# Chunk-selected attention and a gated feed-forward layer on one core: scores of the first batch's four head pairs in two halves of query rows, and a DMA turn for the norm rows of its second half

## The chip, the cores and the metric

The kernel runs on one core of a Trainium2 chip. The metric is the time of one execution on the device in microseconds (us), as the median of several runs; lower is better. A core has five engines that work side by side, each in its own fixed order: TensorE (PE, matrix products and transposes), VectorE (DVE), ScalarE (ACT), GpSimd (POOL) and SyncE (SP, which here only issues DMAs). DMA engines move data between DRAM and the on-chip memory SBUF. Matrix products land in PSUM, a small memory of eight banks.

## The reference: what is computed

There are 4 batches, 8 heads, 768 positions and a head dimension of 64. The first part is attention in which every query row keeps only six chunks of 32 keys, chosen by an upper bound on the scores:

```python
k_min, k_max = min and max of k over each chunk of 32 keys
ub = np.sum(np.maximum(q * k_min, q * k_max), axis=-1)      # per query row and chunk
ub = np.where(causal, ub, -1e9)
top_chunks = np.argsort(ub, axis=-1)[..., -6:]
scores = q @ k.T / np.sqrt(64), masked to top_chunks and to the past
attn = softmax(scores)
x = attn @ v                                               # heads side by side: 3072 x 512
```

The second part works on the 3072 rows of x:

```python
xn = x / sqrt(mean(x * x) + 1e-6) * rms_g
g, val = xn @ w_gate, xn @ w_val                            # 512 -> 1536
out = (g / (1 + exp(-g)) * val) @ w_out                     # 1536 -> 512
```

## The kernel before, in words

The attention part goes by pairs of heads: four pairs a batch, sixteen in all (pair p belongs to batch p // 4). The 768 rows of a pair are six tiles of 128.

*Preparation of a pair* (`prep`). Queries and keys are loaded, turned on TensorE (`kT`, `qT`; the tiles pk and pq, line 525) and copied out of PSUM by ScalarE or VectorE (`kE`, `qE`). VectorE takes chunk minima and maxima (`kmn`, `kmx`), an engine takes relu of the turned queries (`relu`, line 641 or 643), and TensorE multiplies them to the bounds (`ub`, line 731; from pair 6 on two pairs together, line 789). The bounds are copied out (`ubE`), turned back (`up`), masked (`ubm`), and the sixth largest is found (`max`, `sel`). What is selected stands as extra rows beside the queries, so that one product gives the masked scores. For pairs 0 to 2 these rows are turned by TensorE (`selT`, `selC`); from pair 3 on they go through a buffer `qn` of bf16 queries and are turned by DMA from SP's queue (`qX`). The two `qn` buffers are cleared once by VectorE (`qn0`, line 356). POOL casts keys to bf16 (`kC`) and issues the loads of values and of the feed-forward weights wg, wv and wo.

*Scores* (`scores`). The causal triangle of a head is 21 blocks of 128 x 128. They come in groups of at most four blocks: TensorE makes a group of scores (`sc`, line 876; in the first batch also adds the triangular mask, line 882), ScalarE takes the exponentials (`exp`, line 893), TensorE multiplies them with the values (`av`, line 912). When all groups of a head are done, VectorE divides by the sums and writes the rows to xb (`xb`, lines 932 and 933). A pair is done whole (six groups a head) or in two halves of 384 query rows, with two groups for the first half (4 and 2 blocks) and four for the second (4, 4, 4 and 3). Which of the two is set by `PARTS`; before, only pair 3 goes in halves.

*Norm and feed-forward* (`norm`, `ffn`). Both go by halves of a batch, 384 rows. The norm sums squares (`sq`, on ScalarE or VectorE), takes the root on POOL (`root`, line 981), scales the rows on VectorE (`xs`, line 989) and turns them: in batch 0 by TensorE (`tp`, line 1011) with a copy out of PSUM (`tpE`), in the other batches by a DMA from SP's queue (`xT`, line 1000). The feed-forward has twelve groups of four gate matmuls (gp, line 1045), each followed by tanh on ScalarE (line 1052) and a product on VectorE (`tg`), twelve of four val matmuls (vp, line 1066) with another product (`hh`), and nine groups of four output matmuls (po, line 1086).

*Fillers.* `busy` (line 346) emits matmuls on a tile of zeros that nothing reads: 48 of 512 columns from the start on and 40 of 256 columns once the last scores of pair 2 are out (`BUSY, LATER = 48, 40`).

*Order.* Every piece of work is a step with an engine, an assumed duration, a rank and the buffers it opens and uses. A planner in the kernel (`Order.run`) goes through assumed time and gives each free engine the ready step of lowest rank whose buffers are free. The ranks are sums of table entries: `RANK` by kind of step (first batch, later batches), `TIMES` by the place in the problem (s0.3 is the second half of the scores of pair 0, n0.1 the norm of the second half of batch 0, f0.1 its feed-forward). Fillers have the highest ranks, so TensorE gets one when nothing else of its own is ready in assumed time. The result is one fixed order an engine. On the chip each engine follows its order and waits where an input or a buffer is not ready.

Of the kernel before, what the change touches and what calls it, by code (L numbers as in the profile page):

```python
# [26 lines left out]
    dict(  # L27
        av=439.71, dif=-349.0, eps=-276.35, exp=56.9, kC=119.11, kE=221.89, kT=-479.5,
        kload=-91.99, kmn=-561.73, kmx=-221.73, max=-117.69, qC=120.39, qE=644.67, qN=97.14,
        qT=303.27, qX=110.23, qload=17.43, relu=-156.64, root=392.56, sc=392.96, sel=176.91,  # L30
        selC=388.0, selT=-168.59, sq=-325.5, tp=-47.15, tpE=460.17, ub=-387.44, ubE=-1000.64,
        ubm=-238.37, up=-379.03, vload=-360.06, xb=-167.37, xs=293.02,
    ),
    dict(
        av=-243.01, dif=-122.81, eps=-968.41, exp=80.0, gate=-57.45, hh=-33.27, kC=474.21,
        kE=54.78, kT=-28.02, kload=327.35, kmn=571.37, kmx=673.95, mask=-6.85, max=351.72,
        out=-338.93, po=268.25, poE=188.61, qE=-4.14, qN=444.8, qT=271.57, qX=-691.62,
        qload=314.07, relu=202.91, root=-1348.37, sc=-186.72, sel=354.08, sq=285.76, tanh=579.3,
        tg=-259.04, ub=-101.04, ubE=-390.25, ubm=307.49, up=-117.99, val=-52.48, vload=103.56,
        xT=119.23, xb=-299.83, xs=-84.52,  # L40
    ),
)

TIMES = {
    "a0": -417.11, "a1": 120.7, "a10": 211.74, "a11": -52.39, "a12": 226.13, "a13": 390.87,
    "a14": 307.84, "a15": 583.2, "a2": -326.55, "a3": -12.31, "a4": -161.66, "a5": -30.78, "a6":
    133.0, "a7": 70.59, "a8": 128.02, "a9": 121.26, "f0.0": 33.65, "f0.1": 8.37, "f1.0": -84.59,
    "f1.1": 458.33, "f2.0": 528.25, "f2.1": 57.29, "f3.0": 75.85, "f3.1": 711.78, "ke": 138.67,
    "ke0": 432.93, "l0": -295.48, "l1": -95.28, "l10": 399.97, "l11": 344.28, "l12": 487.92,
    "l13": 531.58, "l14": 907.9, "l15": 667.8, "l2": 140.89, "l3": 25.16, "l4": -81.25, "l5":  # L50
    119.09, "l6": 9.37, "l7": 156.16, "l8": 243.85, "l9": 217.21, "n0.0": -794.06, "n0.1":
    230.63, "n1.0": -549.93, "n1.1": 453.35, "n2.0": -334.87, "n2.1": 123.71, "n3.0": 67.64,
    "n3.1": 574.2, "pace0": -0.69, "pace1": 11.25, "pacef0.0": 0.39, "pacef0.1": 15.72,
    "pacef1.0": 11.97, "pacef1.1": 14.19, "pacef2.0": 25.48, "pacef2.1": 21.31, "pacef3.0":
    -30.15, "pacef3.1": 4.73, "pacen": -9.51, "qn0": -62.11, "s0.0": -763.02, "s1.0": -94.31,
    "s10.0": 453.73, "s11.0": -82.75, "s12.0": 288.69, "s13.0": 337.03, "s14.0": 103.21,
    "s15.0": 675.54, "s2.0": -261.49, "s3.0": -328.04, "s3.3": -46.56, "s4.0": -161.4, "s5.0":
    -551.5, "s6.0": 217.9, "s7.0": -246.19, "s8.0": -166.64, "s9.0": 57.52, "step": 1.25, "w":
    26.4, "w0": -49.72, "w1": -9.78, "w2": 75.1, "w3": 187.17,
}  # L60
# [141 lines left out]
def kernel(  # L202
# [11 lines left out]
    nc = tc.nc  # L214
# [5 lines left out]
    NT = S // P  # L220
# [23 lines left out]
    WHOLE, HALVES = [(0, NT)], [(0, HB), (HB, HB)]  # L244
    PARTS = [WHOLE] * 3 + [HALVES] + [WHOLE] * (NPAIRS - NP)
    FIRST = 42.0
# [7 lines left out]
    def add(name, engs, occ, rank, *a, **kw):  # L254
        return order.add(name, engs, occ, rank if isinstance(rank, dict) else {"": rank}, *a, **kw)
# [93 lines left out]
    for i in range(BUSY):  # L349
# [3 lines left out]
            for i in range(SLOTS["ku"])]  # L353
    c_sel = [add("selq0", "DVE", 0.38, -90 + i, lambda e, i=i: nc.vector.memset(SELQ[i][:], 0.0))
             for i in range(SLOTS["selq"])]
    c_qn = [add("qn0", "DVE", 0.5, {"qn0": 1.0}, lambda e, i=i: nc.vector.memset(QN[i][:], 0.0))
            for i in range(SLOTS["qn"])]
# [129 lines left out]
    def prep(c, i0, nb, at, lr):  # L487
# [162 lines left out]
        def choose(last, ubm, m8):  # L650
            for j in range(0, nb, 3):
                def top(e, j=j):
                    if m8.tile is None:
                        tile_of(m8, [P, 2, NT, 8] if side_q else [P, NT, 2, 8], FP32, "m8")
                    for x in range(j, j + 3):
                        for h in range(2):
                            y = (h, x) if side_q else (x, h)
                            nc.vector.max(out=m8.tile[:, y[0], y[1], :],
                                          in_=ubm.tile[:, y[0], y[1], 0:max(8, 4 * (i0 + x) + 4)])

                last = add("max", "DVE", 0.33 + 0.05 * j, rank(at, b, "max", j, "step"), top, last, opens=[m8], uses=[ubm])
                last = [last]
# [188 lines left out]
    def scores(c, i0, nb, at, pace, adds):  # L851
# [3 lines left out]
        for hl in range(2):  # L855
# [63 lines left out]

            if p == 2 and hl:  # L920
                for i in range(LATER):
                    bank = Buf("ps")
                    add("busy", "PE", pe(2 * P), 1000.0 + i, busy(bank, 2 * P), [last_sc], opens=[bank])
# [21 lines left out]
    def norm(b, half, at, pace):  # L945
# [38 lines left out]
        for j, i in enumerate(rows):  # L984
# [10 lines left out]

            if b:
                def move(e, i=i, xs=xs):
# [123 lines left out]
    for b in range(B):  # L1121
        for half in range(2):
            norm(b, half, f"n{b}.{half}", "pacen")
            ffn(b, half, f"f{b}.{half}", f"pacef{b}.{half}")
    PLACE.update(TIMES)

# [32 lines left out]
```

## Time and profile before

| | before |
|---|---|
| median of 3 runs | 316.25 us (315.89 to 316.34) |
| the profiled execution | 315.79 us, of which its span is 314.0 us |
| TensorE busy | 308.6 us (98%) |
| VectorE busy | 230.7 us (73%) |
| ScalarE busy | 194.4 us (62%) |
| POOL busy | 100.7 us (32%) |
| granted TensorE clock | 1.0 |
| moved by DMA | 35.36 MB |

A row of the groups view names line, engine and operation, then output<-inputs, the shapes and the count; behind the bar stand the busy time and the mean duration of one, and the idle time just before them with what ended it. A row of the timeline has start and duration (both us), engine, line, operation, count, and in brackets the idle time ahead of it and what ended that. Neighbouring instructions of one kind are merged. Matmuls overlap in the pipeline, so their cost is the distance from start to start, not the duration of one. A row of the windows view gives length and then, for TensorE, its weight loads, VectorE, ScalarE and POOL, the busy time with the count, then clock, DMA share and GB/s. A row of the chain gives start, length and the work that the end of the kernel depends on at that moment. Line numbers are those of the kernel before.

### The profile page before, as it was taken

The page shows a single profiled execution, that of the slowest core. Times are in us where ns is not written, and L with a number is a line of the kernel's source. Part 1 is how long each engine was busy: PE and PEld are TensorE (multiplying, and loading weights), DVE is VectorE, ACT ScalarE, POOL GpSimd, SP SyncE. Part 2 cuts the span into 40 slices and gives each one's busy share as a digit, 9 for nine tenths or more (in the row PEclk, how much of TensorE's full clock was granted, in tenths as well). Part 3 has the DMA queues.
Part 4 walks back from the last instruction along what each step waited for, and adds up shares of the span by engine and source line. Part 5 has one row for each costly group of instructions (what it writes and reads, how often), then busy time and mean ns, then how long its engine had stood idle before and what let it go on. Part 6 is the DMA issues. An engine that isn't in the chain of part 4 may idle for free.

```text
span 314.0 us, 7640 instructions
## 1 busy us (share of the span) xinstructions
PE 308.6 (98%) x2844; PEld 196.1 (62%) x2844; DVE 230.7 (73%) x654; ACT 194.4 (62%) x420; POOL 100.7 (32%) x157
## 2 busy tenths in 40 slices
PE   7999999999999999999999999999999999999995
PEld 4567877666566775666667565656666645655542
DVE  7699986888988487967986799879464663873530
ACT  5589987863475987478579654344988823333321
POOL 8666534342353564045357300001522220000000
PEclk9999999999999999999999999999999999999999
DMA  8999989989989898979934640002341045001102
GB/s 171 210 190 178 145 108 207 198 114 143 196 86 199 126 179 152 201 164 222 158 79 61 93 102 0 2 2 52 84 94 59 20 118 150 3 0 65 38 22 111
DMA packets 113301, 35.36 MB, mean 113 GB/s; under 512 B 106224, under 2 KB 110064, under 8 KB 113264
## 3 DMA queue, kind: packets, MB, share of 16 engines
q1 hardware_dynamic: 83152, 26.62, 40.9%
q0 software_dynamic: 28512, 7.87, 25.6%
q10 hardware_dynamic: 1600, 0.39, 0.6%
q8 instruction: 22, 0.36, 0.5%
q14 instruction: 15, 0.12, 0.1%
HBM read 28.57 MB, written 6.29 MB: 111 GB/s over the span
## 4 chain that ended last, share of the span: by engine, by line
PE 97%; DMA 1%; ACTq 0%; ACT 0%; issue 0%
PE gp L1045 20%; PE vp L1066 20%; PE po L1086 20%; PE sc L876 12%; PE av L912 7%; PE busy L346 4%; PE pq L525 4%; PE pk L525 3%; PE ub L789 2%; PE ub L731 2%; DMA qnat<-in_q_dram 1%; PE up L811 1%; PE sc L882 1%; PE up L755 1%; PE tp L1011 0%; ACTq L505 0%
## 5 line engine op out<-in xcount | busy, mean ns | idle before, releaser
L893 ACT ACTIVATE pt<-sc 128x512 bf16<-128x512 f32 (+2 forms) x192 | 88.4, 578 | 10.1 <-PE sc L876 5.3
L1052 ACT ACTIVATE sg<-gp 128x384 bf16<-128x384 f32 x96 | 47.7, 500 | 62.7 <-PE gp L1045 60.0
L1066 PE MATMUL vp<-xT,wv 128*128 128x384 bf16 x384 | 77.0, 326 | 0.0
L1045 PE MATMUL gp<-xT,wg 128*128 128x384 bf16 x384 | 76.2, 326 | 0.0
L1086 PE MATMUL po<-wo,hh 128*128 128x512 bf16 x288 | 69.3, 379 | 0.0
L1058 DVE SCALAR_TENSOR_TENSOR tg<-sg,gp 128x384 bf16<-128x384 bf16 x96 | 52.2, 548 | 21.7 <-ACT sg L1052 19.5
L1074 DVE TENSOR_TENSOR hh<-vp,tg 128x384 bf16<-128x384 f32 x96 | 51.8, 551 | 11.1 <-PE vp L1066 7.3
L1045 PEld LDWEIGHTS <-wg 128*128 128x128 bf16 x384 | 36.8, 98 | 24.5 <-issue 1.0
L1066 PEld LDWEIGHTS <-wv 128*128 128x128 bf16 x384 | 36.9, 98 | 24.1
L876 PE MATMUL sc<-qs,ke 128*128 128x128 bf16 (+5 forms) x420 | 51.4, 251 | 0.0
L1086 PEld LDWEIGHTS <-hh 128*128 128x128 bf16 x288 | 27.6, 98 | 27.5
L301 POOL CAST ke<-kt 64x768 bf16<-64x768 f32 x31 | 26.4, 852 | 36.9 <-ACT kt L297 17.0
L876 PEld LDWEIGHTS <-ke 128*128 128x128 bf16 (+1 forms) x420 | 30.3, 97 | 11.3 <-issue 1.6
L899 POOL TENSOR_SCALAR_AFFINE_SELECT pt<-pt 128x512 bf16<-128x512 bf16 (+1 forms) x48 | 24.4, 527 | 37.6 <-ACT pt L893 37.4
L912 PEld LDWEIGHTS <-pt 128*128 128x128 bf16 x672 | 28.8, 98 | 7.7 <-POOL ke L301 0.6
L912 PE MATMUL av<-vx,pt 128*128 128x65 bf16 x672 | 32.6, 193 | 0.0
L299 ACT ACTIVATE osb<-po 128x512 f32<-128x512 f32 x19 | 11.4, 602 | 21.4 <-PE po L1086 21.4
L346 PE MATMUL busy<-zeros 128*128 128x512 bf16 (+1 forms) x88 | 20.1, 349 | 1.3 <-DVE zeros L341 1.3
L933 DVE TENSOR_TENSOR xb<-av,rden 128x384 bf16<-128x384 f32 (+1 forms) x34 | 18.1, 534 | 1.2
L989 DVE SCALAR_TENSOR_TENSOR xs<-xb,ri,gains 128x512 bf16<-128x512 bf16 x24 | 16.9, 746 | 2.7 <-DMA xT<-xs 2.1
L301 POOL CAST qn<-qnat 128x768 bf16<-128x768 f32 x10 | 8.2, 821 | 31.9 <-DMA qs<-qn 30.7
L481 POOL DMA_DIRECT2D vx<-in_v_dram x16 | 16.8, 1052 | 4.0 <-PE av L912 2.6
(87 smaller groups left out, 303.1 us busy)
## 6 DMA issues: line engine op xcount, KB each, us to landing
out_dram<-osb SPq DMA_DIRECT2D x24, 256.0 KB, 2.2
knat<-in_k_dram SPq DMA_DIRECT2D x30, 192.0 KB, 4.3
qnat<-in_q_dram SPq DMA_DIRECT2D x30, 192.0 KB, 4.8
vx<-in_v_dram POOLq DMA_DIRECT2D x16, 192.0 KB, 4.7
wg<-in_moe_w_gate_dram POOLq DMA_DIRECT2D x2, 768.0 KB, 8.6
wv<-in_moe_w_val_dram POOLq DMA_DIRECT2D x2, 768.0 KB, 7.8
wo<-in_moe_w_out_dram POOLq DMA_DIRECT2D x2, 768.0 KB, 9.9
qs<-qn SPq DMA_TRANSPOSE x26, 3.3
```

Source lines behind the costliest of these rows:

```text
L301: engine[e].tensor_copy(out_, in_)
L346: nc.tensor.matmul(t[:, 0:n], zeros[:, 0:P], zeros[:, 0:n], start=True, stop=True)
L876: nc.tensor.matmul(t[:, x:x + m, :].rearrange("p a b -> p (a b)"), ke[kk, kb * P:(kb + 1) * P], qs[kk, q0 * P:(q0 + m) * P], start=not tri ...
L893: nc.scalar.activation(out=t[:, 0:nn, :], in_=sc.tile[:, 0:nn, :], func=ACT.Exp, scale=SCALE)
L899: nc.gpsimd.affine_select(out=pt.tile[:, 0:nd, :], in_=pt.tile[:, 0:nd, :], compare_op=ALU.is_ge, fill=0.0, base=0, pattern=[[0, nd], [1, ...
L912: nc.tensor.matmul(av.tile[:, qi - i0, :], pt.tile[:, x, :], VX[c.v.slot][:, hl * NT + kb, :], start=(begin and m == 0), stop=(left[0] == ...
L1045: nc.tensor.matmul(t[:], wg[:, g, hs], XT[b].tile[:, g, cols], start=(g == 0), stop=(g == NP - 1))
L1052: nc.scalar.activation(out=t[:], in_=gp.tile[:], func=ACT.Tanh, scale=0.5)
L1058: nc.vector.scalar_tensor_tensor(out=t[:], in0=sg.tile[:], scalar=1.0, in1=gp.tile[:], op0=ALU.add, op1=ALU.mult)
L1066: nc.tensor.matmul(t[:], wv[:, g, hs], XT[b].tile[:, g, cols], start=(g == 0), stop=(g == NP - 1))
L1074: nc.vector.tensor_tensor(out=t[:], in0=vp.tile[:], in1=tg.tile[:], op=ALU.mult)
L1086: nc.tensor.matmul(po.tile[:], hhs[ht].tile[:, th * P:(th + 1) * P], wo[:, ht, :], start=(ht == 0), stop=(ht == NHT - 1))
```

## The change: what it does

All four pairs of batch 0 now go in two halves. The 40 later fillers wait for the last score group of the second half of pair 2. The norm rows of the second half of batch 0 are turned by DMA from SP's queue instead of by TensorE. The planner's assumed durations of clearing a `qn` buffer and of a group of maxima are raised, the places s0.3, s1.3 and s2.3 are added, and nearly every number in the two tables of ranks is another, so the order of work on all engines differs:

```diff
-        ubm=-238.37, up=-379.03, vload=-360.06, xb=-167.37, xs=293.02,
+        ubm=-390.61, up=-397.31, vload=-301.28, xT=220.85, xb=-318.72, xs=172.54,
...
-    -30.15, "pacef3.1": 4.73, "pacen": -9.51, "qn0": -62.11, "s0.0": -763.02, "s1.0": -94.31,
...
+    -28.83, "pacef3.1": 4.77, "pacen": -12.12, "qn0": -204.68, "s0.0":
+    -858.36, "s0.3": 4.94, "s1.0": -170.21, "s1.3": 225.32, "s10.0": 486.07, "s11.0": -198.16,
+    "s12.0": 334.79, "s13.0": 615.55, "s14.0": -53.83, "s15.0": 697.68, "s2.0": -148.98, "s2.3":
+    74.37, "s3.0": -357.45, "s3.3": 122.85, "s4.0": -43.33, "s5.0": -909.96, "s6.0": 328.66,
...
-    PARTS = [WHOLE] * 3 + [HALVES] + [WHOLE] * (NPAIRS - NP)
+    PARTS = [HALVES] * NP + [WHOLE] * (NPAIRS - NP)
...
-    c_qn = [add("qn0", "DVE", 0.5, {"qn0": 1.0}, lambda e, i=i: nc.vector.memset(QN[i][:], 0.0))
+    c_qn = [add("qn0", "DVE", 0.85, {"qn0": 1.0}, lambda e, i=i: nc.vector.memset(QN[i][:], 0.0))
...
-                last = add("max", "DVE", 0.33 + 0.05 * j, rank(at, b, "max", j, "step"), top, last, opens=[m8], uses=[ubm])
+                last = add("max", "DVE", 0.40 + 0.05 * j, rank(at, b, "max", j, "step"), top, last, opens=[m8], uses=[ubm])
...
-            if p == 2 and hl:
+            if p == 2 and hl and i0 + nb == NT:
                 for i in range(LATER):
...
-            if b:
+            if b or half:
                 def move(e, i=i, xs=xs):
...
+    for p in range(NP - 1):
+        PLACE[f"s{p}.3"] = TIMES[f"s{p}.0"] + 20.0
     PLACE.update(TIMES)
```

In the built order VectorE clears the two `qn` buffers ahead of the zeros tile. Two fillers stand before the first transposes instead of six, and nine of the narrow fillers stand among the score groups of pair 4, behind the first six gate groups. POOL issues the first wo load ahead of the first wv load, and the latter behind the key casts of pair 7.

## The prediction

> **What bounds the kernel now.** I read the page first: busy shares, the slices, and the chain that ended last.
>
> ```profile
> PE 308.6 (98%) x2844; PEld 196.1 (62%) x2844; DVE 230.7 (73%) x654; ACT 194.4 (62%) x420; POOL 100.7 (32%) x157
> PE   7999999999999999999999999999999999999995
> PEclk9999999999999999999999999999999999999999
> PE 97%; DMA 1%; ACTq 0%; ACT 0%; issue 0%
> L346 PE MATMUL busy<-zeros 128*128 128x512 bf16 (+1 forms) x88 | 20.1, 349 | 1.3 <-DVE zeros L341 1.3
> ```
>
> TensorE is busy from the first slice to the last, at full granted clock, and 97% of the chain is TensorE. But 88 of its instructions are fillers, matmuls on a tile of zeros whose result nobody reads. So the stretch before the first gate matmul is not useful work all through; there other engines set the pace and the fillers take up the waiting. The waits of TensorE come next, then the timeline of TensorE and VectorE at the start.
>
> ```profile
> PE busy L346 <- DVE zeros L341: 1.3, 1, 1.3
> PE pq L525 <- DMA qnat<-in_q_dram: 0.3, 1, 0.3
> ```
> ```profile
> 0.93 0.27 DVE L341 MEMSET zeros<- 128x256 uint32 x1 [0.93 <-PEq L1143]
> 1.26 2.74 PE L346 MATMUL busy<-zeros 128*128 128x512 bf16 x6 [1.26 <-DVE zeros L341]
> 2.52 1.75 DVE L356 MEMSET qn<- 128x896 uint32 x2
> 3.79 0.85 PE L525 MATMUL pk<-ident_f,knat 128*128 128x128 f32 x3
> 4.75 0.52 PE L525 MATMUL pk<-ident_f,knat 128*128 128x128 f32 x3
> 9.62 0.65 PE L731 MATMUL ub<-qt,ku 64*32 64x256 f32 x12
> ```
>
> TensorE has only two recorded waits, both before 6 us. After that it issues without a recorded pause until the end. The six fillers from 1.26 to 3.79 take 0.42 each, and the later ones half of that (0.216, below): the first 3.5 us of TensorE's activity run at half rate.
>
> Last the stage where the first gate matmul runs, in the chain and the timeline.
>
> ```profile
> 9.69 1.01 PE ub L731 x24
> ...
> 12.89 2.59 PE busy L346 x12
> ...
> 25.05 1.04 PE av L912 x34
> ...
> 57.87 0.88 PE sc L876 x10
> ...
> 80.00 0.66 PE pk L525 x6
> ...
> 85.21 1.45 PE ub L789 x32
> ```
> ```profile
> 51.08 0.39 PE L1011 MATMUL tp<-ident_b,xs 128*128 128x128 bf16 x4
> 51.30 0.60 PE L346 MATMUL busy<-zeros 128*128 128x256 bf16 x4
> 51.74 0.39 PE L1011 MATMUL tp<-ident_b,xs 128*128 128x128 bf16 x4
> 53.81 2.44 PE L1045 MATMUL gp<-xT,wg 128*128 128x384 bf16 x14
> 55.76 2.11 PE L1045 MATMUL gp<-xT,wg 128*128 128x384 bf16 x12
> 58.59 0.81 PE L1066 MATMUL vp<-xT,wv 128*128 128x384 bf16 x4
> ...
> 61.91 0.81 PE L1066 MATMUL vp<-xT,wv 128*128 128x384 bf16 x4
> ```
>
> The first gate matmul starts at 53.81, and every filler lies ahead of it. Three groups of four fill 53.81 to 55.76, so a gate group takes 0.65; a val group has the same shape. From there to the end TensorE does nothing but useful work. So the time is: the moment T of the first gate, plus all TensorE work behind it, plus whatever TensorE then waits. No later slack exists to absorb a delay.
>
> **The change, part by part.** Where I say what stands where in the new kernel, it is read from its built instructions, engine by engine, which hold no times. The count and widths of the fillers stay: 48 of 512 columns, 40 of 256. That limits the gain at once: a filler is paid whether it covers a wait or not.
>
> *Scores in halves.* A head's exponentials cover the same 21 blocks of 128 in six instructions either way, so ScalarE gains nothing. Score matmuls become 12 more, with the same columns: TensorE 0. Each of six heads of pairs 0 to 2 is normalised twice instead of once:
>
> ```profile
> 42.95 0.17 DVE L932 RECIPROCAL rden<-av 128x3 f32<-128x3 f32 x1
> 43.16 0.36 DVE L933 TENSOR_TENSOR xb<-av,rden 128x192 bf16<-128x192 f32 x1
> 44.40 0.20 DVE L932 RECIPROCAL rden<-av 128x6 f32<-128x6 f32 x1
> 44.63 0.56 DVE L933 TENSOR_TENSOR xb<-av,rden 128x384 bf16<-128x384 f32 x1
> ```
>
> Two halves are 1.06, a whole 0.76: 0.30 x 6 = 1.8 us more on VectorE. In the new order three bound evictions and a mask copy leave VectorE for ScalarE, which more than pays for it, and all first-half rows are normalised before the last second-half scores, so I cost it at nothing. If that cover fails, up to 1.8 goes into T.
>
> *Start.* VectorE now clears the two qn buffers (1.75) ahead of the zeros tile. The zeros are ready at 0.93 + 1.75 + 0.27 = 2.95 instead of 1.20, TensorE's first filler starts near 3.0, and only two run before the first transposes, which stay near 3.8 because the key load sets them. Half rate then lasts to about 6.5. The second key transposes (0.33 at full rate) take 0.64 behind a cold filler and end near 5.56 instead of 5.1; ScalarE's copy and the bounds matmul of pair 0 (9.62) follow. Between 0 (hidden behind another input) and 0.6 (two transposes at double time), I take 0.35.
>
> *Between that bounds matmul and the gate.* Before: 66 fillers, after: 61. Four more are wide (2.59 / 12 = 0.216), nine fewer narrow (51.74 - 51.30 = 0.44 for four, 0.11): +0.86 - 0.99 = -0.13. The rest is equal work (the transposes of pair 7's keys change places with pair 5's queries, 0.66 each). So T = 53.81 + 0.35 - 0.13 = 54.03, if other engines keep up as before.
> Do they? The TensorE work in this stretch adds up to: 22 transposes of 0.33, five bounds of 1.01 and five turns of 0.33, three selection turns (taken like those), 216 score and mask blocks of 0.055 (0.88 / 16), 168 products of 0.031, three turns of 0.22 and 9.98 of fillers, 42.7 us in 53.81 - 9.62 = 44.2. So TensorE loses 1.5 us in small pieces. Bounds on T: 1.5 earlier, or 1.8 later by the VectorE price.
>
> *Behind the gate.* Nine narrow fillers now stand between the scores of pair 4: +0.98. Twelve transposes of the second norm half go to the DMA: three times 51.30 - 51.08 = 0.22, -0.66, with one eviction each off ScalarE or VectorE, which were not the bound.
>
> *A wait that appears.* In the old order the twelve score groups of pair 4 alternate with four val matmul groups (the first and last vp rows stand above), so TensorE works while ScalarE takes the exponentials. In the new one the first wv load is issued only behind the key casts of pair 7 on POOL, and the order puts six gates, then the twelve score groups with nine fillers and two query transposes, then the bounds of pairs 6 and 7, and val only behind these. The bounds wait for the relu of pair 7, and ScalarE has that behind six tanh and ten exponentials:
>
> ```profile
> 57.26 0.49 ACT L1052 ACTIVATE sg<-gp 128x384 bf16<-128x384 f32 x1 [0.16 <-PE gp L1045]
> 57.91 0.49 ACT L1052 ACTIVATE sg<-gp 128x384 bf16<-128x384 f32 x1 [0.16 <-PE gp L1045]
> 58.30 4.68 ACT L893 ACTIVATE pt<-sc 128x512 bf16<-128x512 f32 x10
> 36.54 0.84 ACT L641 ACTIVATE rt<-qt 128x768 f32<-128x768 f32 x1
> ```
>
> The same six tanh and ten exponentials stand in the old order. Each tanh waits for its gate (0.65 apart), and the ten end at 62.98, T + 9.17. The relu ends 0.7 to 0.84 later, so the bounds can start at about T + 10.0. TensorE has until then 6 x 0.65 + 42 x 0.055 + 0.98 + 0.66 = 7.85. It stands 2.15 us, and val, gates and every po queue behind it in order. That is the main term. A lower bound is 0.5 (if ScalarE ran its 6 x 0.49, 4.68 and 0.84 without a pause from the end of the first gate, T + 0.65, the bounds would start at T + 9.1, less 0.7 of overlapping ends), an upper one 3.5 (the two rmsnorm sums that now sit on ScalarE between the last eviction and the first tanh, 0.7 each, fully on the path).
>
> *The turn by DMA.*
>
> ```profile
> xT<-xs SPq DMA_TRANSPOSE x18, 2.4
> wv<-in_moe_w_val_dram POOLq DMA_DIRECT2D x2, 768.0 KB, 7.8
> 119.76 3.83 SPq L1000 DMA_TRANSPOSE xT<-xs  x3
> 49.30 2.78 SPq L505 DMA_DIRECT2D knat<-in_k_dram  x2
> ```
>
> On SP's queue the first turn follows pair 7's query load, then come pair 9's key load (2.78) and two more turns (1.3 each). Issued from about T + 5, they land near T + 5 + 1.3 + 2.8 + 2.6 + 2.4 = T + 14.1. The gates that read them start at 10.0 + 1.45 + four val groups 2.6 + two turns 0.66 = T + 14.7: hidden, with 0.6 to spare, thanks to the stall in front. Between 0 and +2.4 (one landing), I take 0. The queries and keys queued behind (pairs 9 and 5) are used ten microseconds later or more. The wv load, issued near T + 0 (a wo load now goes ahead of it on POOL's queue, some 15 us earlier) and 7.8 long, makes T + 11.5 with 3 us to spare.
>
> *Sum.* +0.35 - 0.13 + 0.98 - 0.66 + 2.15 = +2.7 us. The profiled execution took 315.79 (span 314.0 and 1.8 around it), 0.46 below the median of 316.25. So 318.5 for a profiled run, and 318.95 against the median.
>
> **A rule against the trace.** After its idle start TensorE ran at half rate from the first filler (1.26) to the second key transposes (4.75): 3.5 us, worth 1.75. What gap brings the half rate back, the trace can't show, for it has no gap that long later. The Trainium skill, "TensorE: Matmul & The Clock Gate", section "HAM oscillation — how this bites in real kernels", says that idle gaps over about 3.4 us put the matmul clock back to half. By that rule the forecast's gap adds nothing, and the gap at its upper bound adds the last rival below.
>
> **Rivals.** Measured differences under 0.2% (0.63 us) can't be told from no change.
>
> *No stall (about 316.8).* If ScalarE reaches the relu as TensorE reaches the bounds, what remains is +0.35 - 0.13 + 0.98 - 0.66 = +0.54. For it: ScalarE's earlier idle. Against it: the 0.16 idle before each tanh shows them bound to the gates, and the order of ScalarE is fixed.
>
> *Faster (about 315.0).* First-half rows of all pairs are ready earlier, so the norm chain no longer ends the stretch ahead of the gate, and the 1.5 us lost there in pieces vanish. With a stall of less than about 0.3 that gives 316.25 + 0.54 - 1.5 = 315.3, or 315.0 if the start costs nothing. It decides only if the stall is nearly absent.
>
> *A second full engine (about 320.5).* In the new order 36 exponentials of pairs 5, 9 and 8 run one after another on ScalarE, six heads at 2.55 (4.68 covers nine long ones and a short one), 15.3, with a relu, a sum and four copies some 18 us, in a stretch that holds 18.3 us of TensorE work by the units above. The densest stretch of before:
>
> ```profile
> 100.00:120.00 20.00, 20.00 (x213) 13.77 (x211) 13.95 (x31) 17.76 (x42) 11.31 (x17) 1.00 1.08 169
> ```
>
> ScalarE was 89% busy there and TensorE full. Near 98% each hand-over shows, and 1 to 2 us of waits would come on top.
>
> *Late rows (about 320.8).* If a turn by DMA lands a whole 2.4 late, the first gates of the second half wait 1.8.
>
> *Half rate again (about 322.1).* If the gap at pair 4 is at its upper bound of 3.5 and TensorE falls back to half rate as at the start: 316.25 + 0.54 + 3.5 + 1.75. It needs both rmsnorm sums on the path; T's early norm chain speaks against that.
>
> **How the numbers follow.** The forecast, one stall near 2 us: 46%. No stall: 16%, its times lying on both sides of 316.88, half same, half slower. Faster: 12%. Second engine full: 14%. Late rows: 8%. Half rate: 4%. That gives 0.12 faster, 0.08 same, 0.80 slower. The predicted time is 318.9. The range leaves out most of the faster case and the tail beyond the upper rivals: 316.0 to 321.6. The likeliest case's own range is 317.8 (half the stall) to 320.2 (stall at its upper bound).
>
> **What would show it.** The zeros memset should end near 2.95 and the first filler follow; the first gate should stand at 53.5 to 54.6; in the waits of TensorE a new row should name the bounds (L789 moved by the edit) waiting for ScalarE's relu, about 2 us; nine fillers should lie behind the gate; three more turns by DMA, twelve fewer tp matmuls. I am wrong if TensorE runs from the gate to the bounds in under 8.3 us, if T lies under 53 or over 55.5, or if a wait later than 80 us is longer than the one at pair 4.

## The result, and the profile after

The kernel after takes 319.81 us in the median of four executions (318.35 to 320.34), beside 316.22 (four, 315.89 to 316.34) before: a ratio of 1.0114, with a 95% interval of 1.0097 to 1.013. It is slower, and its own executions spread over 2.0 us where those of before spread over 0.45. The profiled execution of after took 319.87 (span 318.2), that of before 315.79: 4.08 us more.

First lines of the page of after: busy time, the granted clock, the chain, the fillers.

```profile
PE 308.3 (97%) x2823; PEld 197.1 (62%) x2844; DVE 234.2 (74%) x665; ACT 192.7 (61%) x417; POOL 102.4 (32%) x158
PEclk9999999999999999999999999999999999999999
PE 94%; ACT 2%; DMA 2%; issue 1%; DVE 1%; SPq 0%; ACTq 0%
L347 PE MATMUL busy<-zeros 128*128 128x512 bf16 (+1 forms) x87 | 20.8, 347 | 3.2 <-DVE zeros L342 3.1
```

TensorE's busy time and its clock have not moved. What is new is in the chain, where TensorE went from 97% to 94%: the loss is time in which TensorE waits. The view of TensorE's waits names the places:

```profile
PE busy L347 <- DVE zeros L342: 3.1, 1, 3.1
PE pq L526 <- DMA qnat<-in_q_dram: 1.6, 1, 1.6
PE ub L790 <- ACT rt L642: 0.3, 1, 0.3
```

The third row is the wait that the forecast was built on. Its 0.3 counts only from the modelled end of the matmul ahead; by the starts of the matmuls, below, the wait costs 1.23. The second row was not in the forecast. The timeline shows the first two places, the start and the stage behind the first gate:

```profile
1.06 1.75 DVE L357 MEMSET qn<- 128x896 uint32 x2 [1.06 <-PEq L1146]
2.81 0.27 DVE L342 MEMSET zeros<- 128x256 uint32 x1
3.14 1.03 PE L347 MATMUL busy<-zeros 128*128 128x512 bf16 x2 [3.14 <-DVE zeros L342]
10.67 0.65 PE L732 MATMUL ub<-qt,ku 64*32 64x256 f32 x12
```
```profile
54.58 4.06 PE L1046 MATMUL gp<-xT,wg 128*128 128x384 bf16 x24
59.06 4.68 ACT L894 ACTIVATE pt<-sc 128x512 bf16<-128x512 f32 x10
62.71 1.15 PE L790 MATMUL ub<-qt,ku 64*32 64x384 f32 x16
63.38 0.93 PE L790 MATMUL ub<-rt,ku 64*32 64x384 f32 x8
63.51 0.96 ACT L642 ACTIVATE rt<-qt 128x768 f32<-128x768 f32 x1
64.61 0.85 PE L790 MATMUL ub<-rt,ku 64*32 64x384 f32 x8 [0.30 <-ACT rt L642]
65.39 1.47 PE L1067 MATMUL vp<-xT,wv 128*128 128x384 bf16 x8
```

The first bounds come at 10.67 instead of 9.62, and the first gate at T = 54.58 instead of 53.81. ScalarE ends the relu of pair 7 at 64.47, T + 9.9, as forecast. But TensorE does not stand still until then: 24 of the 32 bounds matmuls read the queries, or the relu of pair 6, and go ahead. Only eight wait. Without the wait the 32 take 1.45 and the values would start at 64.16; they start at 65.39, so the stall is 1.23 and not 2.15.

The place that the forecast missed is in batch 1, at the transposes of pair 14's queries (timelines of TensorE and of SP's queue):

```profile
144.63 0.81 PE L1046 MATMUL gp<-xT,wg 128*128 128x384 bf16 x4
147.09 0.52 PE L526 MATMUL pq<-ident_f,qnat 128*128 128x128 f32 x3 [1.64 <-DMA qnat<-in_q_dram]
```
```profile
134.75 5.53 SPq L1001 DMA_TRANSPOSE xT<-xs  x3
140.38 0.53 SPq L1102 DMA_DIRECT2D out_dram<-osb  x1
141.00 1.06 SPq L506 DMA_DIRECT2D qnat<-in_q_dram  x2
```

SP's queue issues in order. The load of pair 14's queries stands behind three norm turns of batch 1, whose issue took 5.53 here, and an output. The queries land near 147, and TensorE, in order too, has val and gate work behind the transposes that need them.

Against the profiled execution of before, the difference is made up so: T +0.77; nine fillers and stall +0.98 + 1.23; transposes that left TensorE -0.66; pair 14 +1.64. The sum is +3.96 of 4.08.

### The profile page after: what moved, and what is told of

It reads as the page before. It is cut to its first block, busy times and chain, and to the rows that moved or that the text cites. A ratio compares the mean times of both kernels' runs of the same rounds, so it can differ in the third digit from the quotient of the medians.

```text
span 318.2 us, 7636 instructions
## 1 busy us (share of the span) xinstructions
PE 308.3 (97%) x2823; PEld 197.1 (62%) x2844; DVE 234.2 (74%) x665; ACT 192.7 (61%) x417; POOL 102.4 (32%) x158
## 4 chain that ended last, share of the span: by engine, by line
PE 94%; ACT 2%; DMA 2%; issue 1%; DVE 1%; SPq 0%; ACTq 0%
PE vp L1067 19%; PE gp L1046 19%; PE po L1087 19%; PE sc L877 11%; PE av L913 7%; PE busy L347 5%; PE pk L526 4%; PE pq L526 3%; PE ub L790 2%; PE ub L732 2%; DMA qnat<-in_q_dram 2%; ACT pt L894 1%; PE up L812 1%; PE sc L883 1%; PE up L756 1%
## 5 line engine op out<-in xcount | busy, mean ns | idle before, releaser
L894 ACT ACTIVATE pt<-sc 128x512 bf16<-128x512 f32 (+3 forms) x192 | 87.5, 591 | 4.4 <-PE sc L877 4.4
L1046 PE MATMUL gp<-xT,wg 128*128 128x384 bf16 x384 | 75.1, 326 | 0.0
L1087 PE MATMUL po<-wo,hh 128*128 128x512 bf16 x269 | 65.4, 379 | 1.0
L877 PE MATMUL sc<-qs,ke 89*128 89x128 bf16 (+5 forms) x431 | 54.9, 248 | 0.0
L900 POOL TENSOR_SCALAR_AFFINE_SELECT pt<-pt 128x512 bf16<-128x512 bf16 (+1 forms) x48 | 26.2, 562 | 39.6 <-ACT pt L894 39.4
L913 PEld LDWEIGHTS <-pt 128*128 128x128 bf16 x672 | 32.3, 98 | 9.5 <-issue 1.2
L913 PE MATMUL av<-vx,pt 128*128 128x65 bf16 x672 | 38.0, 194 | 0.1
L934 DVE TENSOR_TENSOR xb<-av,rden 128x384 bf16<-128x384 f32 (+1 forms) x40 | 19.1, 478 | 1.4
L990 DVE SCALAR_TENSOR_TENSOR xs<-xb,ri,gains 128x512 bf16<-128x512 bf16 x24 | 18.8, 815 | 1.4 <-DMA xT<-xs 1.1
L659 DVE MAX8 m<-ubm 128x8 f32<-128x8 f32 (+4 forms) x192 | 16.8, 160 | 0.0
```

The costliest lines, as they stand in the source:

```text
L877: nc.tensor.matmul(t[:, x:x + m, :].rearrange("p a b -> p (a b)"), ke[kk, kb * P:(kb + 1) * P], qs[kk, q0 * P:(q0 + m) * P], start=not tri ...
L894: nc.scalar.activation(out=t[:, 0:nn, :], in_=sc.tile[:, 0:nn, :], func=ACT.Exp, scale=SCALE)
L900: nc.gpsimd.affine_select(out=pt.tile[:, 0:nd, :], in_=pt.tile[:, 0:nd, :], compare_op=ALU.is_ge, fill=0.0, base=0, pattern=[[0, nd], [1, ...
L913: nc.tensor.matmul(av.tile[:, qi - i0, :], pt.tile[:, x, :], VX[c.v.slot][:, hl * NT + kb, :], start=(begin and m == 0), stop=(left[0] == ...
L1046: nc.tensor.matmul(t[:], wg[:, g, hs], XT[b].tile[:, g, cols], start=(g == 0), stop=(g == NP - 1))
L1087: nc.tensor.matmul(po.tile[:], hhs[ht].tile[:, th * P:(th + 1) * P], wo[:, ht, :], start=(ht == 0), stop=(ht == NHT - 1))
```

## The experiments

Most edits act on the finished order: `done` is the list that the planner returns, `find(kind, place, n)` is the n-th step of a kind at a place, `move(step, ahead)` takes a step out and puts it ahead of another.

The executions of one program spread over 0.7 us (a_mend) to 4.8 us (a_all), so the profiled executions are compared by marks as well. The profiled execution is often not a middle one: it is the slowest of its program in a_vals (319.17), a_zeros (319.48), a_turn14 (319.41) and a_swap (318.88), and the fastest in a_fill (317.65) and a_relufill (316.78). So the marks tell what happened in that execution, and not what a median is made of. The table is worked out from the traces (start of the first matmul of each kind; all in us): first bounds of pair 0; first gate T; from T to the first gate of batch 1; from there to the end of TensorE. The last column is how long after the first filler TensorE ran at full rate, taken as the first of three successive matmuls that start 0.22 (512 columns) or 0.11 (128 columns) apart, and not twice that; a first gap of up to 0.29, in which the change itself falls, is counted in, so the moment is known to about 0.3.

| kernel | median, and against before on the same chip | first bounds | T | to batch 1's gates | from there to the end | full rate after |
|---|---|---|---|---|---|---|
| after | 319.81, +3.59 | 10.67 | 54.58 | 88.11 | 171.82 | 4.5 |
| a_vals | 317.83, +1.91 | 10.46 | 54.38 | 88.89 | 170.54 | 4.0 |
| a_load | 318.33, +2.41 | 11.25 | 55.16 | 90.05 | 169.98 | 5.9 |
| a_zeros | 318.73, +2.81 | 11.33 | 55.25 | 88.11 | 170.76 | 8.0 |
| a_all | 320.68, +4.76 | 10.30 | 54.21 | 91.28 | 169.98 | 6.0 |
| a_start | 317.88, +1.97 | 8.70 | 54.70 | 88.11 | 170.26 | 3.6 |
| a_turn14 | 318.42, +2.51 | 10.68 | 54.59 | 89.44 | 169.99 | 4.5 |
| a_swap | 317.78, +1.87 | 11.23 | 55.14 | 88.39 | 169.99 | 5.8 |
| a_fill | 318.46, +2.62 | 10.29 | 54.21 | 88.11 | 169.98 | 3.9 |
| a_relufill | 317.34, +1.50 | 9.83 | 53.87 | 87.42 | 170.13 | 2.9 |
| a_mend | 318.75, +2.91 | 11.13 | 55.04 | 88.25 | 169.98 | 5.5 |

Two things are read from it ahead of the single edits. From batch 1's gates to the end TensorE needs 169.98 when nothing waits; after needed 1.84 more in its profiled execution; six other programs that change nothing there needed 0 to 0.8 (a_vals 0.56, a_zeros 0.78, a_start 0.28, a_swap 0.01, a_fill 0, a_relufill 0.15). And from the first bounds to T lie 43.91 or 43.92 in nine of the eleven rows (44.04 in a_relufill, 46.00 in a_start; 44.19 before), while the first bounds themselves come at 9.83 to 11.25 in the eight programs that start with the very same instructions.

### Values ahead of the bounds (a_vals)

```diff
+    move(find("wv", "w0"), find("wo", "w2"))
+    for n in range(2):
+        move(find("val", "f0.0", n), find("ub", "a7"))
```

> The changed kernel with two moves in its order: the first wv load goes ahead of the first wo load on POOL's queue, and two val groups of the first half go ahead of the bounds of pairs 6 and 7 on TensorE. Theory A (two waits of TensorE plus a late start make the loss): the 1.2 us gap between the halves of those bounds is filled by 1.3 us of val work, so about 1.2 us less than the changed kernel, 318.6 us. Theory B (halving itself and the turn by DMA make the loss, wherever the order puts things): no difference, 319.8 us.

Measured 317.83 (ratio 1.0071, interval 1.0044 to 1.0099). The wait at pair 4's bounds is gone from TensorE's waits, but two others are there behind the first gate:

```profile
PE pq L526 <- DMA qnat<-in_q_dram: 1.0, 1, 1.0
PE up L812 <- ACT ubd L298: 0.6, 1, 0.6
```

From T to batch 1's gates it is 0.78 longer than after. Pair 7's queries now land late, at 61.05 instead of 53.67: the wo load is issued right behind the wv load, and in a_swap, where it is not, they land at 54.04. And the turned bounds (up) wait for ScalarE's copy, which the two val groups had covered in their old place. So what is gained does not come from the stall: the profiled execution is 0.70 shorter than that of after, since T is 0.20 earlier and pair 14 waits 1.28 less, against these 0.78.

### Pair 14's queries loaded sooner (a_load), or turned later (a_turn14)

```diff
+    move(find("qload", "l14"), find("xT", "n1.0"))           # a_load
```
```diff
+    move(find("qT", "a14", 0), find("gate", "f1.0", 6))      # a_turn14
+    move(find("qE", "a14", 0), find("tanh", "f1.0", 6))
```

> The changed kernel with pair 14's query load ahead of the three norm turns of batch 1 on SP's queue. Theory A: TensorE no longer waits 1.64 us for it at 145 us, so 318.2 us, unless the norm turns, then about 1 us later, make the first gates of batch 1 wait (then 319 us). Theory B: no difference, 319.8 us.

> The changed kernel with the first query transposes of pair 14 (and their copy on ScalarE) three gate groups later in the order of TensorE; SP's queue stays. Theory A: the 1.64 us wait at 145 us goes, since the query load lands before it is used, 318.2 us. Rival: the stage is short of transfers as a whole, and the wait moves to the next thing loaded, 319.5 us or more.

Measured 318.33 (ratio 1.0103, 1.0062 to 1.0144) and 318.42 (1.0084, 1.0061 to 1.0106). In both, pair 14 waits for nothing: 169.98 and 169.99 from batch 1's gates on, 1.84 less than after. This agrees with the load as the cause, but does not prove what the edits are worth, since programs without them waited 0 to 0.8 as well. In a_load's profiled execution (320.56, one of two near 321 beside three near 318) the turns, now behind the load, are what is late instead. The row of its timeline names VectorE's scaling of the next rows, which ends at the same moment, but the gates read the turned rows, and the last of these lands at 145.08:

```profile
145.21 1.46 PE L1046 MATMUL gp<-xT,wg 128*128 128x384 bf16 x8 [1.74 <-DVE xs L990]
```

In a_turn14 the first gates of batch 0's second half wait, of which the edit changes nothing. Row of its timeline, and the landing times of the three turns there and in after (view of the tile xT up to 75 us):

```profile
70.01 1.46 PE L1046 MATMUL gp<-xT,wg 128*128 128x384 bf16 x8 [1.17 <-DMA xT<-xs]
DMA to landing us min/median/max: 3.5/5.0/6.8
```
```profile
DMA to landing us min/median/max: 3.3/3.4/4.5
```

The same three turns, issued at the same time after T, landed up to 2.3 later. This is the rival "late rows": absent in after's profiled execution, 1.17 here, 0.45 in a_swap.

### The start (a_zeros, a_start)

```diff
+    move(find("zeros", None), find("qn0", None))             # both
+    for n in range(4):                                       # a_start alone
+        move(find("busy", None, 17 - n), find("kT", "a0"))
```

> The changed kernel with the zeros tile cleared ahead of the two qn buffers, so that TensorE's first filler starts near 1.3 us again. Theory A: TensorE reaches full rate earlier and the first bounds start near 9.8 instead of 10.67 us, so about 0.8 us less, 319.0 us. Rival: two fillers and then a pause do not count as activity, full rate comes at the same 7.4 us, and the time stays at 319.8 us.

> The changed kernel with the start of the kernel before: zeros cleared first, and four wide fillers moved ahead of the first key transposes (six stand there again), none added. Theory A: full rate comes near 4.8 us as before, the first bounds start at 9.5 to 9.7 instead of 10.67, the first gate about 1 us earlier, 318.8 us, with a smaller spread. Rival: the stretch to the gate is set by other engines, and the gate stays at 54.5 us and the time at 319.8.

Measured 318.73 (ratio 1.0098, 1.0081 to 1.0115) and 317.88 (1.0069, 1.0044 to 1.0093). Timelines of TensorE, a_zeros and then a_start:

```profile
1.25 1.03 PE L347 MATMUL busy<-zeros 128*128 128x512 bf16 x2 [1.25 <-DVE zeros L342]
3.62 0.87 PE L526 MATMUL pk<-ident_f,knat 128*128 128x128 f32 x3 [1.33 <-DMA knat<-in_k_dram]
7.79 0.85 PE L526 MATMUL pq<-ident_f,qnat 128*128 128x128 f32 x3
11.33 0.65 PE L732 MATMUL ub<-qt,ku 64*32 64x256 f32 x12
```
```profile
1.25 2.74 PE L347 MATMUL busy<-zeros 128*128 128x512 bf16 x6 [1.25 <-DVE zeros L342]
8.70 0.65 PE L732 MATMUL ub<-qt,ku 64*32 64x256 f32 x12
10.09 0.84 PE L526 MATMUL pk<-ident_f,knat 128*128 128x128 f32 x6 [0.24 <-DMA knat<-in_k_dram]
54.70 1.63 PE L1046 MATMUL gp<-xT,wg 128*128 128x384 bf16 x9
```

Two fillers at 1.25 and then a pause bring nothing: three transposes at 7.79 still take 0.85, and the bounds come at 11.33 (10.30 in a_all, which starts in the same way), beside 10.69 in the mean of the eight programs with the late zeros. Six fillers without a pause bring the bounds to 8.70, ahead of before. Yet T is 54.70. TensorE, now ahead, waits for key and query loads and for copies until 23 us, and the 1.97 gained at the start over after is lost again. The start therefore sets T only as long as TensorE is late for everything else; a_relufill, whose bounds came at 9.83, shows the first sign of that limit (T = 53.87, 44.04 behind). The executions of a_start spread over 1.6 us, hardly less than the 2.0 of after.

### First wv and wo loads exchanged (a_swap), and three repairs at once (a_all)

a_swap exchanges the two loads in POOL's order, so that the wo load stays where the wv load was, and moves the two val groups as a_vals does. a_all is a_vals, a_load and a_zeros together.

> Two val groups ahead of the bounds of pairs 6 and 7 as in a_vals, but the first wv and wo loads change places, so that the wo load stands where wv stood. Theory A: the gap of 1.2 us at the bounds is filled and pair 7's queries are not held up by an early wo load, 318.5 us. Rival: pair 7's query load is late again and 0.7 us of the gain are lost, 319.2 us.

> All three moves in one. Theory A: the terms add up, 1.2 + 1.6 + 0.8 = 3.6 us less, 316.2 us, the time of the kernel before. Theory B: 319 us or more.

Measured 317.78 (ratio 1.0055, 1.0035 to 1.0075) and 320.68 (1.0148, 1.008 to 1.0217). In a_swap the values do start at T + 8.2 and no bounds wait, but the copy of the bounds is uncovered then (0.63), and the next gates wait for turned rows (0.45): 88.39 to batch 1's gates, 0.28 more than after. Filling the stall with values gained nothing in this execution; the cover went from one place to another, and the rows were late. a_all has one of the earliest first gates and the longest way from there to batch 1's. Three of its waits:

```profile
PE gp L1046 <- DMA xT<-xs: 2.0, 1, 2.0
...
PE pq L526 <- ACT pt L894: 1.2, 1, 1.2
PE up L812 <- ACT ubd L298: 0.6, 1, 0.6
```

The first is at the first gates of batch 1, as in a_load. The second stands at pair 7's query transposes, as in a_vals: the row names ScalarE, but the second query load lands at 61.07, just ahead of the transposes at 61.16, and not at 53.67 as in after. The repairs do not add up: two of them bring one transfer forward and another is late for it (pair 7's queries with the wo load ahead, the turns with pair 14's load ahead), and the copy that the val groups covered is uncovered.

### The turn by DMA alone, in the kernel before (b_dma)

```diff
+            if b == 0 and half:
+                def over(e, i=i, xs=xs):
+                    nc.sync.dma_start_transpose(
+                        out=XT[0].tile[:, :, i * P:(i + 1) * P], in_=xs.tile[:])
+                OVER.append((x, over))
...
+    for x, over in OVER:
+        done.remove(find("tp", "n0.1"))
+        done.remove(find("tpE", "n0.1"))
+        x.emit = lambda e, old=x.emit, over=over: (old(e), over(e))
```

> The kernel before with one part of the change alone: the second norm half of batch 0 turned by DMA, twelve transposes and three copies less, everything else in the old order. Theory A: TensorE saves 0.66 us and the turns are in time, 315.6 us. Rival: the three turns on SP's queue hold up the key and query loads of pairs 5 and 7 behind them, TensorE waits 1 to 3 us near 64 us, 317 to 319 us.

Measured 316.69 beside 315.91: ratio 1.0029, interval 1.0019 to 1.0039. Timelines of SP's queue and TensorE:

```profile
58.68 1.20 SPq L1016 DMA_TRANSPOSE xT<-xs  x1
59.92 1.20 SPq L505 DMA_DIRECT2D qnat<-in_q_dram  x2
69.86 0.84 PE L525 MATMUL pq<-ident_f,qnat 128*128 128x128 f32 x6 [1.48 <-DMA qnat<-in_q_dram]
```

The twelve transposes leave TensorE, worth 0.66, and the query load, now behind two of the turns, is late by 1.48: the queue stands until the rows of the first turn are there (56.17), and the load is issued at 59.92 instead of 52.12. From T to the end TensorE takes 257.45 instead of 256.42: 1.03 more, of which -0.66 and +1.48 make 0.82. So the wait is the rival's (1 to 3 us expected), and the time lies just below the rival's 317.

### Fillers and relu behind the first gate (a_fill, a_relufill)

```diff
+    late = done.index(find("gate", "f0.0"))                  # both
+    for s in [s for s in done[late:done.index(find("ub", "a7"))] if s.name == "busy"]:
+        done.remove(s)
+    find("relu", "a7").eng = "DVE"                           # a_relufill alone
```

> After without the nine fillers that stand between pair 4's scores, behind the first gate and ahead of pair 7's bounds (0.98 us in the prediction's sum). Prediction's sum, in which fillers and wait are separate terms: 0.98 us less, 318.8 us. Rival: ScalarE runs tanh and ten exponentials one after the other, so pair 7's relu ends 9.9 us behind the first gate with or without the fillers; TensorE only waits longer: the second half of the bounds again starts 10.0 us behind the first gate, and the time stays at 319.8 (319.4 to 320.2).

> As the run before, and pair 7's relu on VectorE, which idled for 2.57 us in that place, instead of ScalarE. If ScalarE's row of ten exponentials is the cause of the wait, the second half of the bounds starts as soon as VectorE's copy of the queries (62.97) and a relu of 0.56 are done, about 9.0 us behind the first gate instead of 10.0, and the first values 9.5 us behind it instead of 10.8: 1.3 to 1.4 less, 318.4 us. What is late next is then the transfer that turns the second half's norm rows, so the gates that read it may wait for up to 1.5 us and give the gain back: 318.4 to 319.8. If the cause is another, the values stay at 10.8 us behind the first gate.

Measured 318.46 (ratio 1.0083, 1.0065 to 1.0102) and 317.34 (1.0047, 1.0034 to 1.006). Timeline of TensorE and SP's queue in a_fill:

```profile
54.21 2.11 PE L1046 MATMUL gp<-xT,wg 128*128 128x384 bf16 x12
64.24 0.85 PE L790 MATMUL ub<-rt,ku 64*32 64x384 f32 x8 [0.30 <-ACT rt L642]
65.02 1.47 PE L1067 MATMUL vp<-xT,wv 128*128 128x384 bf16 x8
144.91 0.49 PE L526 MATMUL pq<-ident_f,qnat 128*128 128x128 f32 x3
134.36 4.00 SPq L1001 DMA_TRANSPOSE xT<-xs  x3
```

Without the nine fillers the last bounds start at T + 10.03 and the values at T + 10.81, exactly as in after; batch 1's gates are 88.11 behind T in both. The fillers cost nothing: ScalarE's chain sets this moment, and fillers and stall are one term of 2.21, not two. The profiled execution is shorter than that of after (317.65) for other reasons: full rate sooner (T 0.37 earlier), and the three turns of batch 1 issued in 4.00 and not 5.53, so that pair 14's queries cost nothing, though the program there is the same. If the fillers cost nothing, the two kernels should take equal times, so their medians, 318.46 (317.65 to 319.82) and 319.81 (318.35 to 320.34), also tell how far a median of few executions of such a kernel can be off.

With the relu on VectorE the values start at T + 10.13: 0.68 less, half of what was expected. VectorE's row of scaled rows and copies is the next limit (timeline of VectorE in a_relufill):

```profile
60.60 1.20 DVE L990 SCALAR_TENSOR_TENSOR xs<-xb,ri,gains 128x512 bf16<-128x512 bf16 x1
61.73 0.55 DVE L302 COPY qt<-pq 128x384 f32<-128x384 f32 x1
62.31 0.77 DVE L644 TENSOR_SCALAR rt<-qt 128x768 f32<-128x768 f32 x1
```

The relu ends at T + 9.21, and the values follow 0.92 behind it. The 0.69 stays gained to batch 1's gates (87.42), without a wait for turned rows.

### All repairs behind the gate (a_mend)

```diff
...
+        f.name, f.emit = "tp", turn          # three of the nine fillers: TensorE turns of n0.1
+        done.remove(find("xT", "n0.1", 0))
...
+        done.remove(s)                       # the other six fillers
+    find("relu", "a7").eng = "DVE"
+    move(find("qT", "a14", 0), find("gate", "f1.0", 6))
+    move(find("qE", "a14", 0), find("tanh", "f1.0", 6))
```

> After with all that showed as a wait behind the first gate taken out: relu of pair 7 on VectorE, six of the nine fillers dropped and the other three replaced by the TensorE transposes of the second half's norm rows (copied by ScalarE, so nothing of batch 0 is turned by DMA), and the queries of pair 14 turned three groups of gates later. If the rest of the loss lies in these places: -1.3 (wait) and -1.65 (pair 14), 316.8 us, and no wait of the gates for turned rows; what is left over the kernel before is then the later first gate (0.8). If the halves themselves cost TensorE time elsewhere, it stays above 318.

Measured 318.75 (ratio 1.0087, 1.0074 to 1.01), worse than expected by 1.9. Nothing waits from batch 1 on (169.98), but T came at 55.04, since full rate came 5.5 after the first filler, and the values only at T + 10.95. ScalarE's copies of the turned rows now stand between its exponentials, and TensorE's next turn waits for them:

```profile
62.90 0.38 PE L1164 MATMUL tp<-ident_b,xs 128*128 128x128 bf16 x4 [0.25 <-ACT xT L298]
```

The relu ends at T + 8.99, early enough, but TensorE reaches the bounds only at T + 9.15, behind these turns (in after at T + 8.13): what the relu was to give went into turning the rows. The time stays above 318, as the rival said, but not for the rival's reason: from T to the end TensorE takes 258.23, 1.81 more than before, and its work from T to the values (six gates 3.9, scores 2.3, six transposes of queries 0.66, twelve of rows 0.66, bounds 1.45) makes 9.0 of the 10.95. What is left over lies ahead of the values.

### The first gate's chain shortened, in the kernel before (b_xs)

```diff
+    last_xb = find("xb", "s3.3", 1)
+    for n in range(3):
+        move(find("xs", "n0.0", n), last_xb)
...
+    for s in run[-8:] + [s for s in done[tp:gate] if s.name == "busy"]:
+        done.remove(s)
...
```

> Before with the first gate's chain shortened: VectorE scales the first half's norm rows (ready for it at 49.3) ahead of the last division of pair 3's second half instead of 50.1, ScalarE copies the turned rows ahead of the squares of the second half (one of which goes to VectorE), and thirteen fillers ahead of the first gate are dropped. If that chain, and not the work of TensorE, sets the first gate, it comes at 52.3 instead of 53.8 and the time is 314.5 us (314.3 to 315.5); if what follows (the second half's norm rows, the loads) sets the end, it stays at 315.9; if the squares hold up the first tanh, it loses up to 0.6.

Measured 316.85 beside 315.84: ratio 1.0033, interval 1.0021 to 1.0045. VectorE does scale the rows from 49.43, but TensorE stops between the turns (timeline of TensorE):

```profile
50.36 0.39 PE L1011 MATMUL tp<-ident_b,xs 128*128 128x128 bf16 x4
52.05 0.61 PE L346 MATMUL busy<-zeros 128*128 128x256 bf16 x4 [1.30 <-DVE xb L933]
54.33 4.06 PE L1045 MATMUL gp<-xT,wg 128*128 128x384 bf16 x24 [0.69 <-ACT xT L297]
```

A filler, too, needs a PSUM bank, and its bank held the products that the postponed division was to read. So whether that chain alone sets the first gate stays open. No kernel of this study is faster than before.

## Why the prediction was right, and where its steps were not

The forecast was 318.9 (316.0 to 321.6), slower by way of one stall at pair 4's bounds. The median is 319.81: the sign and the range hold, the mechanism is there, but it is about a third of the loss and not most of it. Two of the forecast's own signs of being wrong also came: the first bounds started 8.13 behind the gate and not 8.3 or more, for the reason given below at the stall, and a wait later than 80 us, that of pair 14, was longer than the one at pair 4 (1.84 by the marks, beside 1.23). T, at 54.58, lay where it was forecast. That the time came out near the forecast is in part luck. By the steps:

*Start, +0.35: mis-sized; +1.05.* The zeros tile and the first filler came as read from the order (3.14, two fillers). The step took half rate to last the 3.5 that the profile of before shows and so to end near 6.5. It ended at 7.66, 4.5 behind the first filler, and in the eight programs with this same start at 2.9 to 5.9. The extremes of these, a_relufill and a_load:

```profile
6.06 0.49 PE L526 MATMUL pq<-ident_f,qnat 128*128 128x128 f32 x3
9.83 0.65 PE L732 MATMUL ub<-qt,ku 64*32 64x256 f32 x12
```
```profile
8.02 0.85 PE L526 MATMUL pq<-ident_f,qnat 128*128 128x128 f32 x3
11.25 0.65 PE L732 MATMUL ub<-qt,ku 64*32 64x256 f32 x12
```

Query transposes that stand at full rate in one are still at half rate in the other. The mean of the first bounds over the eight is 10.69, so +1.05 is the usual value and not bad luck. The start of before varies too: in the three programs that begin with its instructions (before, b_dma, b_xs) full rate came about 3.5, 3.1 and 5.2 behind the first filler and the first bounds at 9.62, 9.37 and 9.95, in the mean 9.65. One profile could not show that. The Trainium skill, "TensorE: Matmul & The Clock Gate", section "Part 1: The HAM clock gate (the "warmup" mystery)", says that full rate comes after at least one busy window of about 3.4 us and that the windows run free of the kernel's start, with a variation of 0.5 us either way. That the moment varies between executions of the same instructions agrees with these runs; the size does not, for here it is 3.0 us from end to end, and the measurement decides. Where a window began, no run here shows.

*Bounds to gate, -0.13: right; -0.28.* 43.91 instead of 44.19. Halving the scores, priced at nothing, cost nothing here. That the first gate is earlier by the norm chain (the rival "faster") did not happen. With the old start and the new halves TensorE came no sooner to T than 54.70 (a_start), but that run moved fillers too; halving alone was not tried, since the planner's tables belong to one division of the work.

*Nine fillers +0.98 and stall +2.15: one term; 2.21.* The moment at which ScalarE ends the relu was right to 0.1 us. Two errors stood behind it: all 32 bounds matmuls were taken to need that relu, and only eight do (the values came at T + 10.81 and not T + 11.45); and the fillers were paid beside the stall in the sum, though they were also counted within TensorE's 7.85 up to the bounds. The second is only apparent: the gap was taken as what is left when the fillers are done, so fillers and gap make 3.13 against before, and a_fill shows that without the fillers the same moment comes. What was too large is the gap, by 0.92: 0.64 for the values that came sooner, and 0.28 because TensorE needed 8.13 up to the bounds and not 7.85. That a filler is paid whether it covers a wait or not does not hold at this place.

*Transposes, -0.66: right,* as b_dma shows within 0.2 beside its wait.

*Turn by DMA, hidden with 0.6 to spare: right in the profiled execution, thin as said.* The last turned rows landed at T + 12.91, and the gates came at T + 14.08 without a wait. In a_turn14 and a_swap they waited 1.17 and 0.45, so "late rows" does happen with this order in some executions.

*Missing: pair 14's queries, +1.64 in the profiled execution (1.84 by the marks).* The step that failed is the reading of SP's queue. It followed the moved turns of batch 0 and the loads next to them, and took the rest of the order to be as before. The new tables had also put a query load of batch 1 behind three turns and close to its use. The rows of the queue and of TensorE show the cause in that execution. Over the seven profiled executions with this part unchanged the marks give 0 to 1.84, in the mean 0.5, so it belongs to the spread of after more than to its typical time.

*The other rivals.* No second full engine: from batch 1's gates on nothing is left to explain once pair 14 is served, and TensorE has no recorded wait between 66 and 140 us in after. No half rate again: the 24 gate matmuls ahead of the gap at pair 4 take 0.163 each (54.58 to 58.48) and the eight val matmuls behind it 0.164 (65.39 to 66.70). The gap was 1.23 and never near the 3.5 of that rival, whose sum makes 322.0 and not 322.1.

Against the profiled execution the sum was 1.37 too low: 0.92 too much for the stall, 0.70 too little for the start, 0.15 too much between bounds and gate, 1.64 left out for pair 14, and 0.1 that no row explains. With pair 14 at its mean of 0.5 the errors nearly cancel, so a right time is no proof of the single terms here.

## What to carry to other kernels

When an engine runs full and in order, price a wait by the instructions that truly need the late input, not by the whole group they stand in, and count fillers and stall as one term up to the moment another engine sets. When a change rewrites an order by tables, go through each DMA queue for every load that now stands behind a turn or an output and ask when it is used, in the stages that the change does not name too. A repair that lets the full engine arrive sooner is worth only as much as the next transfer or copy is early, and one that brings a transfer forward can make another late; here three repairs together gained nothing.

## What was not expected of the hardware

The same first instructions reached full matmul rate 2.9 to 5.9 us after the first filler, and two fillers followed by a wait of 1.3 us or more did not shorten it (8.0 in a_zeros, 6.0 in a_all). The three transposing DMAs of batch 1 in SP's queue took 4.00 to 5.53 us to issue in unchanged programs, and the three of batch 0 landed after 3.3 to 4.5 us in one execution and 3.5 to 6.8 in another. In the profiled executions T varies by 1.29 us with the moment of full rate (53.87 to 55.16 in the eight programs with the same start) and pair 14's wait by 1.84. That is enough for the spread of 2.0 us of the kernel after, but which of them made it is not shown, since only one of its executions was profiled.
